# Forty empty instructions each on ScalarE and SyncE behind the GLU product of a decode block

## The chip, the cores and the metric

One core of a Trainium2 chip. The metric is the device time of one execution in microseconds (us), as a median of runs. The profile's span runs from the kernel's first to its last recorded instruction and is some 1.2 to 1.4 us shorter than the metric in the kernel before: the metric also holds part of what the trace's record of semaphore updates shows behind the last instruction: one semaphore counts up, the others are reset, and the first counts up again. I call this the teardown.

## The reference

A decode step for one token: layer norm, attention over a cache of 32 heads x 4,096 positions, residual, layer norm, gated MLP, residual.

```python
h  = x + attention(layernorm(x), k_cache, v_cache, wq, wo)      # 32 heads, 4096 positions, D = 640
g, u = layernorm(h) @ w_gate, layernorm(h) @ w_up               # 640 -> 1728
h2 = h + (gelu(g) * u) @ w_down                                 # 1728 -> 640
```

## The kernel before

The kernel streams 84 MB of cache and weights through SBUF. `P.op` appends a function to the list of one engine, with the operations it depends on; waits and semaphores are made from that. The part at issue is its last one: the GLU product `hm` on VectorE, the down product on TensorE, which waits for `w_down` piece by piece, the copies of the output row by VectorE and ScalarE, and its transfer by SyncE.

```python
g9 = V(lambda e: e.tensor_mul(hm[:, :], gu[:, :], ps_u[:, 0:15]), g6, up)

def idle(eng, n):
    def fn(e):
        for _ in range(n):
            i = e.nop(hint="n", nofuse=True)
        return i
    return P.op(eng, fn)
idle("vector", 12)
# ... (down: 4 matmuls for each of 15 blocks of w_down) ...
T(down([13, 14]), g9, d_wp)
T(down(range(4)), d_wd[0])
T(down(range(4, 8)), d_wd[1])
T(down(range(8, 12)), d_wd[2])
dn = {q: T(down([12], [q]), d_wd[3]) for q in (0, 2, 1, 3)}
os = [V(lambda e, q=q: e.tensor_copy(out_row[0:1, 160 * q:160 * q + 160], ps_d[32 * q:32 * q + 1, 0:160]), dn[q])
      for q in range(2)]
os += [A(lambda e, q=q: e.copy(out_row[0:1, 160 * q:160 * q + 160], ps_d[32 * q:32 * q + 1, 0:160]), dn[q])
       for q in range(2, 4)]
d_out = P.dma("sync", out[0, :, :], out_row[:, :], *os)
P.op("sync", None, d_out)          # SyncE's last instruction: the wait for the output's landing
```

An empty instruction computes nothing: the profile lists it as a NOP with no operand (its form is "-"). Twelve of them stand in VectorE's stream already.

The softmax here doesn't subtract the row's maximum and nothing guards it: scores larger than these inputs give would overflow.

## Time and profile before

| | before |
|---|---|
| device time | 202.65 us (202.62 to 202.75) |
| span of the profiled execution | 201.5 us |
| last piece of `w_down` lands | 198.74 us |
| output issued by SyncE | 200.36 us |
| SyncE's last instruction, the wait for the landing | 201.51 us |
| teardown, from that wait to the last hop of the second round | 1.44 us |

Times of rows are counted from the span's start. The lines on the tail of the kernel stand in the prediction. The last row is not in any of the profile's tables: it is read from the trace's record of semaphore updates, where one semaphore (number 2) counts up nine times in each of two rounds, from 199.885 to 201.799 and from 202.591 to 202.948 us. Between the rounds, from 201.759 to 202.367, the others are reset. I call each count a hop; the recorded texts call a round a barrier. No record names the engine of a hop; I name it by its place in time.

Four more names stand for records only. A stall is one distance between the starts of two instructions of an engine that is far longer than its neighbours (462 ns on VectorE, where the others are 46 to 47), or a like time behind SyncE's last wait (0.526 us more than before). Its place in the engine's stream is a crossing. The stretch between two crossings is a block; only `sync_168_early` shows two on one engine, 128 instructions apart, the second by its late hop. A fetch is a packet on a queue of kind "instruction": inside the span q14's one packet is of 8,192 bytes, and q8's four are of 16,384. That a fetch brings the instructions of a further block is my reading of the names and the times, and no record shows it.

### The profile page before, as it was taken

Reading aid. Unit: us, or ns where it says so; the run is one execution under the profiler, and the core shown is the slowest. Engines: PE = TensorE matmul, PEld = TensorE weight load, DVE = VectorE, ACT = ScalarE, POOL = GpSimd, SP = SyncE. Lnnn points to the kernel's source line nnn. Section 1 sums busy time; section 2 is a strip of 40 time slices with the busy share of each in tenths; the row PEclk is TensorE's granted clock in tenths of the full one; section 3 lists DMA queues with packets and bytes.
Section 4 is the critical chain, followed back from the end, with each engine's and each line's share of the span. In section 5 each row is a group of like instructions: output and inputs, shape, how many; then the busy total and the mean of one; then the engine's idle time right before and its main releaser. Section 6 shows DMA issues by size and latency. Waiting matters only on the chain.

```text
span 201.5 us, 2014 instructions
## 1 busy us (share of the span) xinstructions
PE 122.1 (61%) x1008; PEld 34.7 (17%) x756; DVE 100.9 (50%) x51; ACT 12.6 (6%) x33; POOL 34.4 (17%) x36
## 2 busy tenths in 40 slices
PE   0108019759908953692469439907780789479685
PEld 0101000002200120102010201100120022169583
DVE  0200196885199169608950796199229901420321
ACT  2100000001000100010001001000100010010101
POOL 6400000000063008002600170053007200100000
PEclk9999999966985995899559957975998569855555
DMA  9999999999999999999999999999999999999992
GB/s 358 415 411 455 423 429 416 429 442 455 420 429 423 423 423 475 429 416 429 423 429 423 475 423 416 429 423 429 449 449 423 423 429 408 439 420 425 411 408 80
DMA packets 3849, 84.31 MB, mean 418 GB/s; under 512 B 450, under 2 KB 644, under 8 KB 1156
## 3 DMA queue, kind: packets, MB, share of 16 engines
q1 hardware_dynamic: 3842, 84.23, 97.7%
q8 instruction: 4, 0.07, 0.1%
q14 instruction: 1, 0.01, 0.0%
q10 hardware_dynamic: 2, 0.00, 0.0%
HBM read 84.23 MB, written 0.00 MB: 418 GB/s over the span
## 4 chain that ended last, share of the span: by engine, by line
DMA 68%; PE 19%; DVE 9%; SPq 3%; issue 1%; DVEq 0%
DMA v_slot<-in_A_v_cache_dram 42%; DMA k_slot<-in_B_w_down_dram 14%; DMA k_slot<-in_A_k_cache_dram 12%; PE psum L363 9%; PE psum L167 8%; DVE prod L375 6%; SPq L59 3%; DVE sc L381 2%; PE psum L352 1%; PE psum L525 0%; DVE out_row L534 0%; DVEq L114 0%
## 5 line engine op out<-in xcount | busy, mean ns | idle before, releaser
L375 DVE TENSOR_TENSOR prod<-k_slot,qb 128x8192 bf16<-128x8192 bf16 x16 | 75.2, 4737 | 6.8 <-DMA k_slot<-in_A_k_cache_dram 4.7
L167 PE MATMUL psum<-prod,id_b 128*128 128x512 bf16 x233 | 67.1, 445 | 0.0
L381 DVE TENSOR_REDUCE sc<-psum 128x128 f32<-128x2048 f32 x8 | 18.3, 2291 | 51.0 <-PE psum L167 51.0
L385 POOL TENSOR_TENSOR p_bd<-pt,own 128x512 bf16<-128x512 bf16 x6 | 28.3, 4715 | 85.3 <-ACT pt L382 85.3
L352 PE MATMUL psum<-prod,id_b 128*128 128x512 bf16 x23 | 10.6, 461 | 49.2 <-DVE prod L375 45.7
L363 PE MATMUL psum<-v_slot,p_bd 128*16 128x512 bf16 x224 | 17.8, 475 | 7.0 <-DMA v_slot<-in_A_v_cache_dram 7.0
L352 PEld LDWEIGHTS psum<-prod,id_b 128*128 128x128 bf16 x23 | 2.3, 99 | 70.3 <-DVE prod L375 47.6
L369 PEld LDWEIGHTS psum<-hs,po_sb 128*128 128x128 f32 x64 | 9.1, 208 | 23.9 <-issue 23.5
L363 PEld LDWEIGHTS psum<-v_slot,p_bd 128*16 128x16 bf16 x224 | 5.8, 105 | 39.7 <-DMA v_slot<-in_A_v_cache_dram 28.0
L392 ACT COPY po_sb<-psum 128x512 f32<-128x512 f32 x7 | 4.1, 586 | 73.6 <-PE psum L363 73.6
L369 PE MATMUL psum<-hs,po_sb 128*128 128x4 f32 x64 | 8.5, 256 | 0.1
L335 PE MATMUL psum<-arena,xlnB 128*32 128x512 bf16 x20 | 3.3, 626 | 7.2 <-DMA arena<-in_A_wq_dram 7.2
L382 ACT ACTIVATE pt<-sc,zero_t 128x128 bf16<-128x128 f32 x8 | 3.2, 401 | 71.1 <-DVE sc L381 71.1
L465 PE MATMUL psum<-aP,arena 128*128 128x1 bf16 x160 | 6.6, 178 | 0.0
L465 PEld LDWEIGHTS psum<-aP,arena 128*128 128x128 bf16 x160 | 6.5, 131 | 0.0
L389 POOL MEMSET spare<- 1x1 f32 x1 | 0.1, 89 | 36.4 <-DVE p_bd L385 36.4
L494 PE MATMUL psum<-hlnT,v_slot 128*128 128x1 bf16 x150 | 5.5, 173 | 0.8 <-issue 0.8
L340 DVE CAST qb<-psum 128x512 bf16<-128x512 f32 x1 | 0.7, 692 | 10.1 <-PE psum L167 10.1
L494 PEld LDWEIGHTS psum<-hlnT,v_slot 128*128 128x128 bf16 x150 | 5.3, 120 | 1.5 <-issue 0.9
L363 PE MATMUL psum<-k_slot,p_bd 128*16 128x512 bf16 x32 | 2.9, 520 | 2.8 <-DVE p_bd L385 2.8
L308 PE MATMUL psum<-one_bf,x_row 1*128 1x1 bf16 x5 | 0.4, 177 | 6.8 <-DMA x_row<-in_A_x_dram 6.8
L311 DVE COPY xx<-psum 128x5 f32<-128x5 f32 x1 | 0.2, 165 | 7.2 <-PE psum L308 7.2
(72 smaller groups left out, 34.8 us busy)
## 6 DMA issues: line engine op xcount, KB each, us to landing
k_slot<-in_A_k_cache_dram SPq DMA_DIRECT2D x8, 4096.0 KB, 25.9
v_slot<-in_A_v_cache_dram SPq DMA_DIRECT2D x7, 4096.0 KB, 17.2
arena<-in_A_wq_dram SPq DMA_DIRECT2D x1, 5120.0 KB, 15.2
arena<-in_A_wo_dram SPq DMA_DIRECT2D x2, 2560.0 KB, 35.2
k_slot<-in_A_v_cache_dram SPq DMA_DIRECT2D x1, 4096.0 KB, 26.8
v_slot<-in_B_w_gate_dram SPq DMA_DIRECT2D x1, 2160.0 KB, 23.7
k_slot<-in_B_w_down_dram SPq DMA_DIRECT2D x3, 640.0 KB, 29.2
v_slot<-in_B_w_up_dram SPq DMA_DIRECT2D x1, 1296.0 KB, 26.5
```

The source lines that it names most:

```text
L59: ev = self.op(eng, lambda e: e.dma_start(out, in_), *deps, dma=True, chan=chan)
L167: built = e.matmul(out, lhsT, rhs, start=start, stop=stop)
L335: mm = held if hf else lambda e, *a, **k: e.matmul(*a, **k)
L352: mm = held if n or not first else lambda e, *a, **k: e.matmul(*a, **k)
L363: i = e.matmul(ps_o[a:a + 16, :], p_bd[:, 4 * b:4 * b + 4, :].rearrange("p g j -> p (g j)"), vt[:, 4 * b:4 * b + 4, :], start=(b < 4), sto ...
L369: i = e.matmul(ps_a[:, bass.ds(at, 4)], po_sb[:, 128 * r:128 * r + 128], hs[:, r, :], start=(r == 0), stop=(r == 3))
L375: mults[G, i] = VM(lambda e: e.tensor_tensor(out=prod[:, i, :, :], in0=kt[:, 64 * i:64 * i + 64, :], in1=qb[:, G, :].unsqueeze(1).to_broad ...
L381: reds[G] = VR(lambda e: e.reduce_sum(sc[:, :], ps_f.rearrange("p (g d) -> p g d", d=16), axis=AX.X), folds[G, 1])
L385: blocks[G] = on(lambda e: e.tensor_tensor(out=p_bd[:, :, :], in0=pt[:, :].unsqueeze(2).to_broadcast([128, 128, 4]), in1=own[:, :].unsquee ...
L392: evs[G] = AS(lambda e: e.copy(po_sb[:, :], ps_o), pvs[G])
L465: r = e.matmul(ps_p[:, c:c + 1], wo_sb[:, i, c::5], aP[:, i:i + 1], start=False, stop=(i == 31), skip_group_check=True)
L494: i = e.matmul(ps[:, m:m + 1], ws, hlnT[:, c:c + 1], start=(c == 0 and m == 0), stop=(c == 4), skip_group_check=True)
```

## The change

Forty empty instructions on ScalarE and forty on SyncE, made to wait for `hm`, so that they run while both engines have nothing to do. They compute nothing.

```diff
-    def idle(eng, n):
+    def idle(eng, n, *deps):
...
-        return P.op(eng, fn)
+        return P.op(eng, fn, *deps)
     idle("vector", 12)
+    idle("scalar", 40, g9)
+    idle("sync", 40, g9)
```

## The prediction

The sum of part 2, 1.92 us, was 1.50 us for forty empty instructions and 0.42 us for VectorE's stall (462 - 47 = 415 ns); part 3 has the same sum. The 1.50 was the estimate, and no trace had shown the price on ScalarE or SyncE. With VectorE's distance of 47 ns, which the trace has, forty would be 1.88 us and the sum 2.30, to 199.32; that is still 0.36 us ahead of ScalarE's copy (199.68) and 0.98 ahead of the end of SyncE's wait (200.30), so the argument holds with it. What the first rival needs, 65 and 82 ns, is to be set against VectorE's 47, or 57 with the stall spread over forty. Part 4 put the start of the new fetches at about 199.2, with the same price and VectorE's lag of 1.15 us from stall to fetch, behind the last of `w_down` (198.74) and free; with 47 ns it is 199.5. In the second rival, the hop distances of 34 to 48 ns that it states are those of the first round behind 201.63, and the second round's are 23 to 98.

> **What bounds the kernel now.** I read the page first. Its DMA digits are 9 in 39 of 40 slices and the chain of waits gives DMA 68% of the span: the kernel streams its 84 MB, and the compute engines keep pace. The change sits behind `hm`, the product of the GLU, so only the tail matters. I asked there for the chain in order of time:
>
> ```profile
> 171.27 27.47 DMA k_slot<-in_B_w_down_dram
> 198.74 0.04 issue
> 198.78 0.87 PE psum L525 x20
> 199.65 0.30 DVE out_row L534
> ```
>
> The columns are start, length, what. The last of `w_down` lands at 198.74, 20 matmuls take 0.87 us, the output row is copied, and SyncE sends it. `hm` is long done by then. The timeline of the same stretch says how long (start, length, engine, line; in brackets the idle time before it and its releaser):
>
> ```profile
> 196.83 0.17 DVE L509 TENSOR_TENSOR hm<-gu,psum 128x15 bf16<-128x15 f32 x1 [2.00 <-PE psum L494]
> ...
> 198.78 0.49 PEld L525 LDWEIGHTS psum<-k_slot,hm 128*1 128x1 bf16 x20 [0.47 <-DMA k_slot<-in_B_w_down_dram]
> 199.64 0.66 DVE L534 CAST out_row<-psum 1x160 bf16<-1x160 f32 x2 [2.64 <-PE psum L525]
> 199.68 0.60 ACT L536 CAST out_row<-psum 1x160 bf16<-1x160 f32 x2 [5.55 <-PE psum L525]
> 200.36 0.27 SPq L59 DMA_DIRECT2D out_dram<-out_row  x1
> ```
>
> `hm` ends at 196.83 + 0.17 = 197.00. ScalarE has nothing from there to 199.68. SyncE has nothing either: its queue's waits show that it sat in one wait, L114, for the last copy:
>
> ```profile
> SPq L114 <- ACT out_row L536: 21.0, 1, 21.0
> SPq L114 <- DMA out_dram<-out_row: 0.9, 1, 0.9
> ```
>
> Last I looked at the twelve empty instructions that VectorE has already, which price the new ones (count, then shortest/median/longest in ns, then first and last start):
>
> ```profile
> L515 DVEq NOP  x12: 18/18/18, 196.9 to 197.8; - x12
> ```
>
> Each is recorded as 18 ns, but the distance of their starts counts. In the trace's records they start every 47 ns, except one gap of 462 ns between the seventh and the eighth (197.14 to 197.60). The average over eleven distances is 0.93 / 11 = 85 ns, and I take the 47 ns as the price and the other 415 ns as one separate stall. The queue table gives a candidate for it:
>
> ```profile
> q8 instruction: 4, 0.07, 0.1%
> q14 instruction: 1, 0.01, 0.0%
> ```
>
> The only instruction packet on q14 inside the span is of 8,192 bytes; it starts at 198.29, 1.15 us after the gap opens, and takes 0.46 us. I read the gap as VectorE crossing a block of its instruction stream and ordering the next one. That is argued from the times, as no record names the engine.
>
> [...]after the output's landing at 201.49, one semaphore counts up in steps of 34 to 48 ns from 201.63 to 201.80, the others are reset from 201.76 to 202.37, and a second round of hops runs from 202.59 to 202.95. That matters since the profiled execution is timed at 202.88 us and its span is 201.5: some 1.4 us of the metric lie outside the span, and the end of that teardown fits.
>
> **The change part by part.**
>
> 1. VectorE: nothing. Its twelve instructions are in the kernel before too; the diff only gives the helper an argument for dependencies.
> 2. ScalarE: 40 empty instructions, which wait for `hm`. [...] They also may cross a block: VectorE had 63 recorded instructions before its gap, ScalarE has 35 before the new ones, so if the streams begin alike the crossing comes at about the 28th. I add VectorE's stall of 0.42 us. Sum 1.92 us, from 197.02 (the semaphore record of `hm`) to about 198.94. The copy it must serve begins at 199.68. Left over: about 0.7 us. All of it lies beside the wait for `w_down`.
> 3. SyncE: the same 1.50 + 0.42 us, to about 198.94. Its next needed instruction is the wait that ends at 200.30. Left over: about 1.36 us.
> 4. Instruction fetches: perhaps two more packets of 8 KB. [...] They cost nothing there.
> 5. Semaphores: `hm` is signalled already, for the down product; the two new waits add no signal. TensorE's program, every transfer and their order stay.
>
> On the path that sets the end the sum is 0 us. So the time is that of before, 202.65 us.
>
> **The rivals.**
>
> First, the empty instructions outlast their gap, and become the wait ahead of the copies. That needs (199.64 - 197.02) / 40 = 65 ns each on ScalarE, or (200.30 - 197.02) / 40 = 82 ns on SyncE[...]. VectorE's own average, stall included, is 85 ns. If ScalarE's sequencer took 85 ns a piece, it would be done at 197.02 + 3.40 = 200.42, the copies would be 0.75 us late, and the time 203.4 us. Against it: that average rests on one stall in eleven distances; forty instructions should meet one as well, not four.
>
> Second, the change gains. If ScalarE and SyncE now order a block of instructions in the teardown, and the empty ones bring that forward into idle time, then up to 0.42 us would be saved, or 202.2 us. It is what VectorE's twelve look made for: the gap comes five before their end. Against it: the hops of the barriers in the teardown, at 34 to 48 ns, leave no room for a stall of 0.4 us at these engines, and the semaphore group reset last runs 0.2 us behind the others[...]. The crossing would then lie beyond what is timed.
>
> Third, an extra fetch comes earlier than I think and shares a DMA engine with the last piece of `w_down`. A packet of 8 KB took 0.46 us, and only one of 16 engines would carry it, so the worst is some 0.4 us, or 203.0 us. For it: the last pieces of `w_down` trickle in on one or two engines after 198.0, so the end does hang on a single engine there. Against it: the crossing would have to come in the first few of the 40.
>
> **Range and chances.** The three runs of before lie within 0.13 us. I widen that by the second and third rival, to 202.3 to 203.05; the first rival, at perhaps one in twelve, lies above. Two per cent is 4.05 us. The largest of the rivals, the first at VectorE's average price on both engines, moves the end by 0.75 us. So within 2% has 0.98.
>
> **What would show it.** Forty NOPs on each queue, begun at 197.0, [...]and done by 199.0. The copies on ScalarE still released by the down product, some 35 ns behind VectorE's first. SyncE's wait L114 still ended by the copy at L536. The instruction packets on q14 up from 1 to as many as 3. If SyncE or ScalarE start late against the product's last signal, the first rival holds. If the span is as before and the time still moves, it is the teardown. What would make me wrong in size: a price of an empty instruction above 65 ns, or a fetch that holds the next instruction up for longer than the 0.7 us left over.

## More of the kernel before

One more view of the kernel before will be needed, that of the transfers from 201.3 to 204 us. There are none, so no fetch is recorded in the teardown:

```profile
DMA packets 0, 0.00 MB, mean 0 GB/s; under 512 B 0, under 2 KB 0, under 8 KB 0
```

In the kernel before the second hop, ScalarE's by its place, came 0.107 us after ScalarE's second copy ended, and the fifth, SyncE's by its place, 0.127 us after SyncE's last wait began; the second round ended at 202.95.

## The result, and the profile after

The changed kernel took 203.26 us (203.21 to 203.37, 4 runs) against 202.66 us of the kernel before on the same chip (202.62 to 202.75). The ratio is 1.003, with an interval of 1.0012 to 1.0047. The kernel is 0.6 us slower, which is small, but about four times the spread of either kernel's runs (0.13 and 0.16 us).

The span did not grow; it is 201.4 us. First the empty instructions (count, shortest/median/longest in ns, first and last start), in the changed kernel:

```profile
L515 SPq NOP  x40: 13/13/18, 196.5 to 197.9; - x40
L515 ACTq NOP  x40: 14/14/14, 196.5 to 198.4; - x40
L515 DVEq NOP  x12: 18/18/18, 196.3 to 197.3; - x12
```

The reader is to see that all eighty are over by 198.4, ahead of the copies. Their distances of start, from the trace's records: 39 ns on ScalarE with one gap of 351 ns behind the 28th, 35 to 38 ns on SyncE (44 and 53 for the first two) with no long gap at all. Then the tail, in the timeline of the changed kernel:

```profile
196.31 0.17 DVE L509 TENSOR_TENSOR hm<-gu,psum 128x15 bf16<-128x15 f32 x1 [1.90 <-PE psum L494]
...
199.56 0.66 DVE L536 CAST out_row<-psum 1x160 bf16<-1x160 f32 x2 [3.08 <-PE psum L527]
199.59 0.59 ACT L538 CAST out_row<-psum 1x160 bf16<-1x160 f32 x2 [5.88 <-PE psum L527]
200.28 0.28 SPq L59 DMA_DIRECT2D out_dram<-out_row  x1
```

ScalarE still starts 0.03 us behind VectorE, and SyncE issues the output 0.72 us after VectorE's first copy began, as it did before (200.36 - 199.64). Its chain of waits in order of time has the same pieces too:

```profile
171.37 27.28 DMA k_slot<-in_B_w_down_dram
198.65 0.04 issue
198.69 0.88 PE psum L527 x20
199.57 0.30 DVE out_row L536
```

So nothing within the span explains a slower kernel. The transfers of 201.3 to 204 us do differ (queue, packets, MB, share of the 16 engines); where the kernel before had none, the changed one has

```profile
DMA packets 1, 0.01 MB, mean 3 GB/s; under 512 B 0, under 2 KB 0, under 8 KB 0
q14 instruction: 1, 0.01, 1.2%
```

That is a fetch of 8,192 bytes, which starts at 202.51, behind the kernel's last instruction. The semaphore records say what it goes with:

| from the trace's records, us | before | after |
|---|---|---|
| SyncE's last wait begins | 201.507 | 201.432 |
| fifth hop | 201.634 | 202.085 |
| between the two | 0.127 | 0.653 |
| fifth hop to ninth | 0.165 | 0.163 |
| ninth hop to the second round's first | 0.792 | 0.791 |
| second round | 0.357 | 0.358 |

One interval grew, by 0.526 us, and every other stayed within 2 ns. It lies directly behind the last instruction of SyncE. Of the 0.60 us between the medians this is most; the other 0.07 us is less than the spread of one kernel's runs. The two profiled executions themselves were timed at 202.88 and 203.21 us, only 0.33 us apart. Their last hops are 0.45 us apart, since SyncE's last wait began 0.075 us earlier in the changed one; and the timed end fell 0.07 us ahead of the last hop in the first and 0.19 us ahead in the second, which nothing here explains.

**Theory.** SyncE's stream has crossings at fixed places, as VectorE's and ScalarE's traces show one each (462 ns behind VectorE's 63rd recorded instruction, 351 behind ScalarE's 63rd). At a crossing SyncE stalls for some 0.4 to 0.5 us, and a fetch follows about 1 us later, as it did 1.15 to 1.25 us after VectorE's stall began and 1.01 after ScalarE's. No record names the engine that ordered a fetch; that is taken from the times. Forty instructions moved a crossing to the place right behind the wait for the output, where the later hops come only after SyncE's. **Rivals.** The loss belongs to ScalarE's forty. Or each empty instruction on SyncE costs a little, 0.6 us for forty. Or it is their running late, beside the last weights and just ahead of the output, that does harm.

### The profile page after: what moved, and what is told of

It is laid out like the page before. It is cut to its first block, busy times and chain, and to the rows that moved or that the text cites. A ratio compares the mean times of both kernels' runs of the same rounds, so it can differ in the third digit from the quotient of the medians. Undisturbed runs are those within 1.5% of the kernel's fastest.

```text
span 201.4 us, 2094 instructions
## 1 busy us (share of the span) xinstructions
PE 118.4 (59%) x1008; PEld 33.6 (17%) x756; DVE 100.8 (50%) x51; ACT 12.6 (6%) x33; POOL 30.8 (15%) x36
## 4 chain that ended last, share of the span: by engine, by line
DMA 85%; PE 9%; SPq 4%; issue 0%; DVE 0%
DMA v_slot<-in_A_v_cache_dram 72%; DMA k_slot<-in_B_w_down_dram 14%; PE psum L363 9%; SPq L59 4%; PE psum L527 0%; DVE out_row L536 0%
## 5 line engine op out<-in xcount | busy, mean ns | idle before, releaser
L167 PE MATMUL psum<-prod,id_b 128*128 128x512 bf16 x233 | 64.6, 432 | 0.0
L352 PE MATMUL psum<-prod,id_b 128*128 128x512 bf16 x23 | 10.4, 452 | 51.1 <-DVE prod L375 47.6
L385 POOL TENSOR_TENSOR p_bd<-pt,own 128x512 bf16<-128x512 bf16 x6 | 24.7, 4115 | 91.0 <-ACT pt L382 91.0
L369 PEld LDWEIGHTS psum<-hs,po_sb 128*128 128x128 f32 x64 | 8.3, 191 | 24.1 <-issue 23.5
L369 PE MATMUL psum<-hs,po_sb 128*128 128x4 f32 x64 | 7.7, 244 | 0.4 <-ACT po_sb L428 0.4
L363 PE MATMUL psum<-k_slot,p_bd 128*16 128x512 bf16 x32 | 3.5, 616 | 2.9 <-DVE p_bd L385 2.9
```

The lines of the kernel that those rows point to most:

```text
L167: built = e.matmul(out, lhsT, rhs, start=start, stop=stop)
L352: mm = held if n or not first else lambda e, *a, **k: e.matmul(*a, **k)
L363: i = e.matmul(ps_o[a:a + 16, :], p_bd[:, 4 * b:4 * b + 4, :].rearrange("p g j -> p (g j)"), vt[:, 4 * b:4 * b + 4, :], start=(b < 4), sto ...
L369: i = e.matmul(ps_a[:, bass.ds(at, 4)], po_sb[:, 128 * r:128 * r + 128], hs[:, r, :], start=(r == 0), stop=(r == 3))
L385: blocks[G] = on(lambda e: e.tensor_tensor(out=p_bd[:, :, :], in0=pt[:, :].unsqueeze(2).to_broadcast([128, 128, 4]), in1=own[:, :].unsquee ...
```

## The experiments

Twelve kernels, each built on the changed one and each correct, three rounds each, beside the kernel before on the same chip. They differ in the counts, and two of them in what SyncE's instructions wait for, so the edits are given in a line or two. Hops, gaps and fetches come from one profiled execution of each kernel.

### Which engine: `scalar_only` and `sync_only`

```diff
-    idle("sync", 40, g9)          # scalar_only
-    idle("scalar", 40, g9)        # sync_only
```

> VectorE 12 and ScalarE 40 empty instructions, none on SyncE. Theory (the change cost 0.6 us because SyncE's forty move SyncE's stream so that it crosses an instruction block right behind the output's landing): the time is that of before, 202.65 us within 0.1, the first barrier hop comes 0.13 us after the landing is seen as in the kernel before, there is no instruction packet behind 200 us, and ScalarE still has one gap of 0.35 us among its forty. Rival (ScalarE's forty cost it, by their fetch or by late copies): 203.26 us.

> VectorE 12 and SyncE 40, none on ScalarE. Theory: all of the loss is here, 203.2 us within 0.1; last wait of SyncE to first hop 0.65 us instead of 0.13; an instruction packet of 8 KB about 1.1 us behind the last wait. Rival (ScalarE's part): 202.65 us.

`scalar_only` took 202.79 us against 202.77 of the kernel before, ratio 1.0003 (0.9986 to 1.0020); hop 0.128 us behind the last wait, and no transfer behind 201.3. `sync_only` took 203.19 us, ratio 1.0019 (1.0002 to 1.0036); hop 0.654 us behind, and a fetch at 202.56. In the transfers of 201.3 to 204 us the two differ as the changed kernel and the kernel before do, `scalar_only` first:

```profile
DMA packets 0, 0.00 MB, mean 0 GB/s; under 512 B 0, under 2 KB 0, under 8 KB 0
```

```profile
DMA packets 1, 0.01 MB, mean 3 GB/s; under 512 B 0, under 2 KB 0, under 8 KB 0
q14 instruction: 1, 0.01, 1.2%
```

The loss is SyncE's. ScalarE's forty, gap and fetch included, cost no time that shows.

### More instructions: `sync_48`

```diff
-    idle("sync", 40, g9)
+    idle("sync", 48, g9)
```

> The changed kernel with 48 instead of 40 on SyncE. Theory: the block now ends inside the empty run (about the 43rd), the gap of 0.35 to 0.5 us shows there and is hidden, since SyncE has nothing to do before 200.2; the time goes back to 202.65 us within 0.1 although eight instructions were added. Rival (each empty instruction on SyncE costs, 0.6 us for forty): 203.26 + 8 x 0.015 = 203.4 us.

202.74 us, ratio 0.9998 (0.9981 to 1.0015). Eight more empty instructions removed the loss, so it is no cost per instruction. The view of SyncE's empty instructions:

```profile
L515 SPq NOP  x48: 13/13/18, 196.1 to 198.4; - x48
```

The 47 distances take 2.24 us, or 48 ns on average, where the forty took 37. Most of the difference is a gap of 441 ns, and it lies behind the 43rd, as expected. (A small one of 78 ns behind the 40th is not explained.) It costs nothing there, as SyncE has nothing to do until 200.3. The hop is back at 0.127 us.

This fixes the place. SyncE has 36 recorded instructions ahead of the empty ones, so its crossing is behind its 79th recorded instruction. With forty, instruction 77 is the wait for the copies, 78 the output's issue and 79 the wait for the landing. The next one is the teardown's first.

### When they run: `sync_40_early`

```diff
-    idle("sync", 40, g9)
+    idle("sync", 40)
```

> The changed kernel, but SyncE's forty wait for nothing, so that they run right behind the last weight issue, near 180 us. Theory (their place in the stream counts, not when they run): still 203.26 us within 0.1, with the 0.65 us behind the last wait. Rival (their running beside the end of the weights, or just ahead of the output's issue, costs it): 202.65 us.

They ran from 179.3 to 180.8 us, and the time was 203.31 us, ratio 1.0027 (1.0011 to 1.0044), with the hop 0.653 us behind. So it is their number, and so the place of what follows them, and not the moment at which they run.

### One instruction at a time: `sync_41` and `sync_42`

```diff
-    idle("sync", 40, g9)
+    idle("sync", 41, g9)          # sync_41; 42 in sync_42
```

> The changed kernel with 41 on SyncE. The run with 48 had its long gap between the 43rd and the 44th, so SyncE's block ends after its 79th recorded instruction, and with forty the first instruction behind the wait for the landing was the 80th. Theory: with 41 the block ends between the output's issue and the wait for its landing, where SyncE has 0.9 us to spare, so the time is 202.7 us within 0.1, and the hop comes 0.13 us behind the last wait. Rival (a cost that grows with the number of instructions on SyncE, or starts at about forty): 203.27 us.

> The changed kernel with 42 on SyncE. Theory: the block ends between the wait for the last copy and the issue of the output, on the path: the issue starts 0.4 to 0.5 us later than the 0.064 us behind that wait which it takes elsewhere, the span grows to about 201.9, the time to 203.1 us. Rival (the crossing hides wherever it is not in the teardown): 202.7 us.

With 41 the block ends between the output's issue and the wait for its landing. SyncE has time to spare there (its list of waits has 0.8 us for the landing), and the stall is gone from the time: 202.72 us, ratio 1.0001 (0.9984 to 1.0017), with the hop 0.164 us behind the last wait. The fetch still comes, at 201.61. With 42 it ends between the wait for the copies and the issue. This is the only one of these kernels in which the loss shows inside the span, which is 202.0 us. In its timeline and in its list of waits at L114:

```profile
199.65 0.59 ACT L538 CAST out_row<-psum 1x160 bf16<-1x160 f32 x2 [5.91 <-PE psum L527]
200.72 0.28 SPq L59 DMA_DIRECT2D out_dram<-out_row  x1
```

```profile
L114 SPq EVENT_SEMAPHORE  x2: 17/17/17, 200.3 to 202.0; - x2
```

The reader is to see 200.3 for the wait for the copies and 200.72 for the issue that follows it. The records put these at 200.267 and 200.721: 454 ns apart, where they are 64 in the kernel before. The landing was then seen 1.25 us after the issue started, where it is 1.14 before. I expected the first of these and not the second. The second lies behind the start of the output's transfer: from there to the landing it was 0.49 us, where it is 0.38 before. The fetch, from 201.34 to 201.83, overlaps that transfer at 201.46 here and in none of the other runs; that it delayed the landing is likely and not shown. Together they make 0.50 us, and the time was 203.26 us, ratio 1.0026 (1.0009 to 1.0042).

One empty instruction thus takes the loss away and a second brings it back. No cost that grows with their number does that.

### Deeper into the teardown: `sync_38`, `sync_36`, `sync_20`

```diff
-    idle("sync", 40, g9)
+    idle("sync", 38, g9)          # sync_38; 36 in sync_36, 20 in sync_20
```

> The changed kernel with 38 on SyncE. With 40 the stall came ahead of SyncE's first hop, with 36 behind it. Theory: with 38, two instructions into the teardown, it is either still ahead of the hop (203.26 us, last wait to hop 0.65 us) or between the hop and SyncE's resets (hop at 0.13 us, the resets of the semaphores from 207 up begin 0.4 to 0.5 us late, [...]most of it is hidden: 202.7 to 202.9 us). Rival (in proportion to the number): 203.23 us with neither.

> The changed kernel with 36 on SyncE. Theory: the block ends four instructions deeper in the teardown than with forty. If that is still ahead of SyncE's first hop, 203.26 us again; if it is behind it, the hop comes 0.13 us behind the wait, and SyncE's later part of the teardown shows the stall: its resets, [...]can hide most of it, so 202.7 to 202.9 us. Rival (a cost in proportion to the number): 203.2 us with the hop at its usual place.

> The changed kernel with 20 on SyncE. Theory: SyncE's block then ends 20 instructions into what follows the landing; with 36, four instructions in, the stall had already moved behind the first round of hops, so with 20 it should lie beyond what is timed: 202.7 us within 0.1, the whole teardown as in the kernel before. Rival (half the instructions, half the loss): 202.95 us.

With 38 the hop was at its place, 0.143 us behind the wait, and the stall had moved behind it. The semaphores from 207 up, which are reset 0.125 us after that hop in the kernel before, began 0.650 us after it. In the changed kernel they begin 0.125 us after it too, and the two runs differ in SyncE's count alone, so I take these resets for SyncE's. But the last group to be reset, the lowest numbers, ended at 202.29, when those were at 202.31, and the second round began 0.788 us behind the first, where it is 0.792 in the kernel before. (There the resets from 207 up end at 201.849 and those of the lowest numbers at 202.367, 0.518 us later. That is the lead that the expectations for 36 and 38 count on; whose the lowest numbers are no record says.) The stall was there and hidden: 202.86 us against 202.85, ratio 1.0001 (0.9984 to 1.0018).

With 36 the hops are within 0.02 us of the kernel before, the resets from 207 up last 0.15 us for 0.09, and the fetch starts at 203.09, behind the last hop. The four runs scattered from 202.82 to 203.36 us, ratio 1.0010 (0.9993 to 1.0027), so it is unclear. The profiled run took 203.36 us, which is 0.35 us beyond its last hop, where in all other profiled runs the time ended 0.02 to 0.19 us ahead of it. Why, stays open. It does not look like the stall itself: in the runs with 38, 40 and 42 the fetch starts 1.07 to 1.09 us behind the last SyncE event ahead of the stall, which here gives about 202.0, where the resets from 207 up end (201.99). A stall of 0.5 us there is over before the second round begins at 202.65.

With 20 nothing is left of it: 202.85 us against 202.85, ratio 1.0004 (0.9987 to 1.0020), and no fetch behind 201.3. Half the instructions are not half the loss.

### The size of a block: `sync_168_early`

```diff
-    idle("sync", 40, g9)
+    idle("sync", 168)
```

> The changed kernel with 168 = 40 + 128 on SyncE, waiting for nothing, so that they run near 180 to 186 us. Theory (a block is the 8,192 bytes of one packet[...]): one long gap behind the 43rd, and the next block ends again right behind the last wait: 203.2 to 203.3 us, last wait to first hop 0.65 us, a fetch behind 202 us. Rival (a single crossing at a fixed place, or a larger block): 202.7 us and 0.13 us.

The long gap came behind the 43rd (426 ns), none came later among the 168, and then the hop was 0.569 us behind the last wait, with a fetch at 202.33. The time was 203.13 us, ratio 1.0017 (1.0000 to 1.0034), so by the times alone it is just short of clear. It is slightly under what was expected; the stall was 0.44 us here. So the pattern repeats after 128 instructions, in the one run that tests it.

### The same place on another engine: `scalar_26` and `vector_none`

```diff
-    idle("scalar", 40, g9)
-    idle("sync", 40, g9)
+    idle("scalar", 26, g9)        # scalar_26
```

> 26 on ScalarE, 12 on VectorE, none on SyncE. ScalarE's block ended behind 63 recorded instructions in four traces; with 26 that is right behind its second copy, the place at which the crossing costs SyncE 0.5 us. Theory (only the engine that arrives last pays): ScalarE's first hop comes 0.3 to 0.4 us later than the 0.10 us behind its copy of the kernel before, [...]and the hop of SyncE does not, so 202.7 us within 0.1. Rival (a crossing behind an engine's last work always costs its stall): 203.1 us.

202.68 us, ratio 0.9992 (0.9975 to 1.0008): the time was as expected, but for another reason. The hop taken for ScalarE's was not late; it came 0.108 us after its second copy, where it is 0.107 in the kernel before. There were two fetches on q14 around 198 us, at 198.00 and 198.58, as in `scalar_only`. In the changed kernel the fetch that follows ScalarE's stall starts at 198.58 too, 1.01 us behind the stall's start. So I estimate ScalarE's crossing at about 197.6 here, two microseconds ahead of the copies (199.69) that precede it in the stream. Why it comes ahead of them is not shown. On SyncE it is otherwise: in `sync_42` the stall comes behind the wait (200.267 to 200.721) and not ahead of it. My expectation had overlooked that the two may differ. The run therefore doesn't test whether a late crossing on ScalarE would be hidden.

```diff
-    idle("vector", 12)
-    idle("scalar", 40, g9)
-    idle("sync", 40, g9)          # vector_none
```

> The kernel before without its twelve on VectorE, nothing on the others. Theory: VectorE's block ended after 63 recorded instructions, it now has 58, so the crossing moves some five instructions into VectorE's teardown. [...]Rival (empty instructions on VectorE do nothing or cost a little): 202.6 us with no fetch on q14 behind 200 us.

202.90 us (three of the four runs 202.85 to 202.95, one 203.37) against 202.75, ratio 1.0015 (0.9998 to 1.0033): unclear by the times. (The expectation gave 202.65 us for a crossing that is hidden between two hops, 1.17 us apart, and 203.05 for one that is not. The 1.17 us are those from the fourth hop, 200.464, to the fifth, 201.634; that both are VectorE's no record says.) In the records one interval is longer than in every other run. The fourth hop of the second round, which I take for VectorE's as this kernel differs from the one before in VectorE's stream alone, came 190 ns behind the third, where it is 43 to 45 elsewhere. So the twelve that the kernel has already seem to be worth some 0.15 us: they pull VectorE's crossing out of the teardown into idle time. That is argued from one profiled run, and no fetch was recorded behind it; with a lag of 1.1 us one would start near 203.7, past the last hop (203.02).

## Why the prediction was right or wrong

**The bound and the price: right.** The chain of waits was unchanged. An empty instruction cost 39 ns on ScalarE and 37 on SyncE (1.44 us over 39 distances), so forty cost 1.57 and 1.47 us, stall left out, where the estimate was 1.50 for both. The first rival, which needed 65 ns, did not occur.

**Parts 1 and 2: right.** ScalarE's crossing came behind the 28th, as estimated, and its stall, 351 - 39 = 312 ns where VectorE's 0.42 us had been taken, fell into idle time. Its last began at 198.4, 1.2 us ahead of the copies. `scalar_only` took the time of before.

**Part 3 is the step that failed.** It gave SyncE the same sum, with the crossing taken over from part 2, where it comes at about the 28th "if the streams begin alike". They don't: what held for ScalarE failed for SyncE. ScalarE's and VectorE's crossings are behind 63 recorded instructions, SyncE's behind 79. With forty that is directly behind the kernel's last instruction, in a stretch in which the later hops come only after SyncE's: they came as closely behind it as before, 0.163 us for 0.165. Neither SyncE's gap nor its fetch was anywhere in the trace of the kernel before, so its place could not be read from there, and I put VectorE's in its stead. The term "On the path that sets the end the sum is 0 us" should have been 0.53 us, as the interval behind the last wait measured. The sign that the prediction named for this did come: "If the span is as before and the time still moves, it is the teardown."

**The second rival saw the place but only one direction.** It asked whether the change takes a crossing out of the teardown, and not whether it puts one in. SyncE had 40 recorded instructions left to the end of its block, and neither a stall nor a fetch shows in the teardown of the kernel before. The forty brought the crossing to the teardown's first instruction.

**Part 4 and the third rival.** The fetch taken for ScalarE's began at 198.58 where 199.2 was estimated for both. That was 0.07 us ahead of the last landing of `w_down` (198.65) and not 0.5 us behind it, as part 4 had it, so the order was wrong, but it delayed nothing that could be seen: the landing was at 198.74 in the kernel before. SyncE's came at 202.51, for the reason above.

**The range.** Its upper end, 203.05, was that of a delayed transfer. A stall on the path behind the output, for which VectorE's gap of 0.42 us gave the size, would have made 202.65 + 0.42 = 203.07, and was left out as the crossing was put elsewhere. That the change is within 2% was right.

What stays open: what SyncE does in the stall (in the changed kernel the late hop, at 202.09, comes 0.42 us ahead of the fetch at 202.51, so SyncE did not wait for this fetch); why the same step cost 0.53 us with forty, 0.44 with 168 and 0.39 to 0.40 inside the stream (`sync_42`, `sync_48`); what ends the timed interval with 36; and why SyncE's first crossing comes 16 recorded instructions later than the others'. No version beat the kernel before: where the stall was hidden, the times were those of before.

## What to carry to other kernels

When instructions are added to or taken from an engine that ends the kernel, ask where the stalls of its stream fall, and keep them out of the chain that ends the kernel, which here was the step to the output's issue and what follows the last wait: here one empty instruction more or less was worth 0.5 us. The stalls measured here, an ordinary distance taken off, were 0.31 us on ScalarE, 0.39 to 0.40 on SyncE (`sync_168_early`, `sync_42`, `sync_48`) and 0.42 on VectorE inside the stream, and 0.44 to 0.53 behind SyncE's last wait. The trace of the kernel before shows no crossing for SyncE, and forty recorded instructions further there was one. A row of empty instructions with one long distance between two starts found it (`sync_48`). And compare the metric with the span: when the time moves and the span doesn't, read what follows the last instruction.
